# Gate projection by block products in one more group, chunks outermost in the output stage, and PSUM banks by due time

## Chip, core and metric

The kernel runs on one core of a Trainium2 chip. The metric is device time in microseconds (us) of one execution, lower is better. The time before is 316.57 us, the median of 4 runs (316.33 to 316.61).

## What is computed

The kernel chains a linear attention with cosine weights and a gated feed-forward block. There are 8 batches, 8 heads, 576 positions and a head size of 64, so 4608 tokens of 512 features; the inner width is 1536.

```python
def phi(x, c, s):                       # c, s = cos, sin of pi/2 * pos / 576
    r = np.maximum(x, 0.0)
    return np.concatenate([r * c, r * s], axis=-1)
kv  = einsum('bhsf,bhsd->bhfd', phi(k), v)
z   = sum(phi(k), axis=2)
num = einsum('bhsf,bhfd->bhsd', phi(q), kv)
den = einsum('bhsf,bhf->bhs', phi(q), z)[..., None] + 1e-06
x   = (num / den).transpose(0, 2, 1, 3).reshape(4608, 512)
g   = x @ w_gate
out = (g / (1 + exp(-g)) * (x @ w_val)) @ w_out
```

## The kernel before

**Groups and tiles.** The 4608 tokens are cut into nine groups (`tg` 0 to 8) of 512 tokens, each of four tiles of 128. Group 0 is spelled out in a list of words; the other groups run in a loop. A group has a product stage of 12 blocks of 128 inner features (`fc`) and an output stage. Attention work is spread between the blocks: the tiles of group `tg + 1` are made while group `tg` is in its product stage.

**Order.** The kernel writes the order of the instructions by hand: each engine runs its instructions in the order in which the Python code issues them. Side work goes into a plan: `at(s, f)` puts a function at slot `s`, `slot(s)` runs what is there. A group has 16 slots, 12 in the product stage and 4 in the output stage.

**Gate and value.** In groups 1 to 6, `ffn_mm` (L564) makes gate and value of a block with four matmuls of 512 columns each; ScalarE takes silu of the gate (L570), VectorE (DVE) multiplies by the value into `ht` (L575). In the groups of `GATE` (7 and 8), `ffn_by_quarters` makes the gate of four blocks at a time from seven block products in place of eight, a scheme of Strassen's kind. It has three thirds (`u`), each with products on banks a, b, e and c (L621): b is copied from a and accumulates in several steps, DVE adds a saved product `m7` to it for c (L659), then adds b to `m7` (L668), and ScalarE takes silu of m7, c, a and b (L627). The value products stay four matmuls of 512 columns (L633), and DVE makes `ht` from both (L638, the gating product). The weights' sums come from `gate_weight_sum` (L597), the tokens' sums from `x_sum` (L605).

**Output.** From group 2 on, `out_by_quarters` makes the output the same way, with seven products of 12 matmuls of 256 columns (L786). Its operand sums are made on DVE by `token_sum` (L760, S1 to S4) and `weight_sum`. Evictions are L799, L801, L811, L816 and L827. In the last group, bank b of this stage is two banks.

**Attention.** For a batch, `phi_q` takes relu on ScalarE (L266) and weights on DVE (L283) into `r_q`, and two DMA transposes on SP (`qturn_dma`, L306) turn it into `phit`. `vmul` (L287) weights v; `kv_mm` (L333) multiplies; `kv_out2` (L356) copies it out. `a_tile2` (L448) makes a tile in two banks; `x_of` divides it (L458, L467, L471), and a DMA transpose on SP (L548) makes `xT`. Groups 7 and 8's tokens come from batches 6 and 7.

**Queues.** Loads from the second batch on go on POOL's queue. `load_behind` (L996) first runs a small POOL copy (L998) that reads the turned q of the batch before, so that the load waits for it. Stores (`store`, L708) go on SP's queue, between the DMA transposes; the last group's are split over SP and ScalarE's queue.

**PSUM.** There are eight banks, handed out by `take`. Before group 7 the one used longest ago is taken; from group 7 on (`loose`), a single bank is taken first so that a pair stays free, then by last use in the order of the code.

Of the kernel before, what the change touches and what calls it, by code (L numbers as in the profile page):

```python
# [18 lines left out]
def kernel(  # L19
# [31 lines left out]
    KH = KC // 2  # L51
    GATE = (7, 8)

# [22 lines left out]
    filled = [False] * 8  # L76
    loose = [False]

    def take(n, hold=None, fills=False, seeded=False):

        taken = {x for r in held.values() for x in r}
        if loose[0]:
            free = [b for b in range(8) if b not in taken]
            if n == 1:
                bs = [min((b for b in free if filled[b] or not seeded), key=lambda b: (
                    not any(x != b and x + 1 != b and x + 1 in free for x in free), used[b]))]
            else:
                b0 = min((b for b in free if b + 1 in free), key=lambda b: max(used[b:b + 2]))
                bs = [b0, b0 + 1]
            if hold is not None:  # L90
                held[hold] = bs
            for b in bs:
                filled[b] = fills or seeded
            touch(bs)
            return banks[:, bs[0]] if n == 1 else banks[:, bs[0]:bs[0] + 2]
        free = [b for b in range(0, 8, n) if not any(b <= x < b + n for x in taken)
                and (filled[b] or not seeded)]

        b0 = min(free, key=lambda b: (n == 1 and hold is not None and hold[0] == "o" and b ^ 1 not in taken,
                                      sorted(used[b:b + n], reverse=True)))  # L100
        if hold is not None:
            held[hold] = range(b0, b0 + n)
        filled[b0:b0 + n] = [fills or seeded] * n
        touch(range(b0, b0 + n))
        return banks[:, b0] if n == 1 else banks[:, b0:b0 + n]

    def touch(r):
        now[0] += 1
        for x in r:
            used[x] = now[0]  # L110

    def give_back(hold):
        touch(held.pop(hold))

# [162 lines left out]
    def phi_q(b, g):  # L277

        if g == 0:
# [4 lines left out]
                                in1=tab, op=ALU.mult)  # L284

    def vmul(b, g):
        nc.vector.tensor_tensor(  # L287
# [52 lines left out]
    def kv_out(b, engs=("act", "dve"), js=slice(0, J)):  # L340
        ps = st[b, "kvps"]
        for e, eng in enumerate(engs):
            for i in range(2):
# [3 lines left out]
                    in_=ps[hs, e, js.start * 2 * D1:js.stop * 2 * D1].rearrange("p (y x) -> p y x", x=D1))  # L347

    kv2s = [consts.tile([P, 2, J, 2, D1], BF16, name=f"kv2_{j}") for j in range(2)]

    def kv_out2(b):

        ps = st[b, "kvps"][:, :, 0:4 * J * D1 // 2].rearrange("p e (j w x) -> p e j w x", j=J, w=2)
        for w, eng in enumerate((nc.scalar.copy, nc.vector.tensor_copy)):
            for i in range(2):
                eng(out=kv2s[b % 2][w * D:(w + 1) * D, :, :, i], in_=ps[i * D:(i + 1) * D, :, :, w])  # L356

    def kv_free(b):
        give_back(("kv", b))

# [75 lines left out]

    def a_tile2(t):

        (b0, c0), (b1, c1) = (divmod(2 * t + r, NC) for r in range(2))
        ps = take(2)  # L440
        if b0 == b1:
# [3 lines left out]
        for e in range(2):  # L445
            for g in range(G):
                for ms, b, c, n in parts:
# [4 lines left out]
                    )  # L452
        x_of(t, ps)

# [152 lines left out]
    def ffn_by_quarters(tg, slot_of):  # L607
# [6 lines left out]

        def free(nm):
            give_back(("g", tg, nm))

        def product(to, u, a, x, first):
            for i in range(2):
                for c in range(KH):  # L620
# [8 lines left out]
        def V(u, i, w):  # L629
            fc = 4 * u + 2 * i + w  # L630
            val[u, i, w] = take(1, ("v", tg, fc), fills=True)
            for kc in range(KC):
                nc.tensor.matmul(out=val[u, i, w], lhsT=wv_sb[:, kc, fc * P:(fc + 1) * P], rhs=xT[tg][:, :, kc],  # L633
                                 start=(kc == 0), stop=(kc == KC - 1))

        def mul(u, i, w):
            fc = 4 * u + 2 * i + w
            nc.vector.tensor_tensor(out=ht[:, fc], in0=gates[u, w][:, i], in1=val.pop((u, i, w)), op=ALU.mult)  # L638
            give_back(("v", tg, fc))

# [4 lines left out]
        for u in range(3):  # L645
# [7 lines left out]
            nc.scalar.copy(out=m7, in_=e)  # L653
            free("e")
            V(*((u - 1, 1, 1) if u else (u, 0, 0)))
            done()
            product(b, u, W2, X2, False)
            c = bank("c", seeded=True)
            nc.vector.tensor_tensor(out=c, in0=m7, in1=b, op=ALU.add)  # L659
            product(a, u, A12, B21, False)  # L660
            silu(u, 1, 0, a)
            free("a")
            if u:
                mul(u - 1, 1, 1)
            V(u, 0, 0) if u else V(u, 1, 0)
            done()
            product(b, u, W1, X1, False)
            nc.vector.tensor_tensor(out=m7, in0=m7, in1=b, op=ALU.add)  # L668
            silu(u, 0, 1, m7)
            product(c, u, A22, X4, False)  # L670
            silu(u, 0, 0, c)
            free("c")
            V(u, 1, 0) if u else V(u, 0, 1)
            done()
            if u == 2:
                for n in (1, 2):
                    token_sum(n, 0, 4)
            mul(u, 0, 0)
# [4 lines left out]
            silu(u, 1, 1, b)  # L683
            free("b")
            if u:
                V(u, 0, 1)
            mul(u, 0, 1)
            if u:
                done()
                token_sum(*((3, 0, 4) if u == 1 else (4, 0, 4)))  # L690
        V(2, 1, 1)
# [29 lines left out]

    def ffn_out(t, f0=0, f1=None):

# [13 lines left out]
        else:  # L737
            nc.vector.tensor_single_scalar(out=ob_of(t), in_=ps, scalar=DOWN, op=ALU.mult)
        store(t)

# [26 lines left out]
    def out_by_quarters(tg, slot_of):  # L767

        last = tg == NTG - 1
        t0 = tg * OUT  # L770
        for t in (t0, t0 + 2):
# [11 lines left out]
        def product(to, a, b, first):  # L783
            for i in range(2):
                for kc in range(HC):
                    nc.tensor.matmul(out=to[i][:, 0] if len(to) == 2 else to[0][:, i],  # L786
# [28 lines left out]
        for p_, o_, x_ in each(b, c[0], C22):  # L815
            nc.vector.scalar_tensor_tensor(out=o_, in0=x_, scalar=UP, in1=p_, op0=ALU.mult, op1=ALU.add)  # L816
        token_sum(4, 4, 6)
        slot_of(0)
# [16 lines left out]
        else:  # L835
            for t in (t0 + 2, t0 + 3):
                store(t)
        slot_of(2)
# [3 lines left out]
        for t in (t0, t0 + 1):  # L842
            store(t, *((slice(HD, d_model), (nc.sync, nc.scalar)) if last else ()))
        slot_of(3)
# [151 lines left out]
    def load_behind(b):  # L996

        nc.gpsimd.tensor_copy(out=hold2, in_=phit[b - 1][0:1, :, 0, 0, 0])  # L998
        load(b, "q")
        if b > 3:  # L1000
            load_kv(b)

    def load_kv(b):
# [9 lines left out]
    for n in range(4):  # L1013
        at(SLOTS * (1 + n * (GATE[0] - 1) // 4) + FC + 3, lambda n=n: gate_weight_sum(n))
    for tg in GATE:
        for n in range(4):
            at(SLOTS * (tg - 1) + FC + (2, 2, 3, 3)[n], lambda tg=tg, n=(2, 0, 1, 3)[n]: x_sum(tg, n))
    for b in range(2, B):
        s0 = SLOTS * (b - 1)
        keng = "dve" if b == 2 else "act"  # L1020
        steps = [lambda b=b, g=g: phi_q(b, g) for g in range(G)]
        steps += [lambda b=b, g=g: (relu_k(b, g, g + 1, keng), vmul(b, g)) for g in range(G)]
        if b == 2:
            fs, tq = [s0 + i for i in (0, 0, 1, 1, 4, 5, 5, 6)], (s0 + 2, s0 + 2)
        else:
            p0 = s0 - SLOTS
            fs, tq = [p0 + 12, p0 + 12] + [p0 + 11 + i for i in range(2, 8)], (p0 + 15, p0 + 16)
            if b == 3:
                fs, tq = [p0 + 12 + i for i in range(4)] + [s0 + 4, s0 + 4, s0 + 5, s0 + 5], (s0 + 2, s0 + 2)
            at(p0 + 3 if b < 5 else p0 + 1, lambda b=b: load_behind(b))  # L1030
        tk = (s0 + 4, s0 + {2: 8, 3: 7}.get(b, 5))
        for s, f in zip(fs, steps):
            at(s, f)
        for e in range(2):
            at(tq[e], lambda b=b, e=e: qturn_dma(b, e))
        at(tk[-1], lambda b=b: kv_mm(b), lambda b=b: kv_out2(b))
        at(tk[-1] + 1, lambda b=b: kv_free(b))
    for t in range(2 * OUT, NTG * OUT):
        tg, i = divmod(t, OUT)
        s = SLOTS * (tg - 1) + (5 if tg > 2 else 4) + 2 * i  # L1040
        if t == 2 * OUT:
            at(s, a_(t, 0))
            at(s + 1, a_(t, 1), turn(t))
        elif tg == 2:
            at((9, 10, 11)[i - 1] + SLOTS, lambda t=t: a_tile2(t), turn(t))
            if i == 2:
                at(11 + SLOTS, load_3)
        else:
            if t in (13, 14, 15):
                s = SLOTS * 2 + t - 4  # L1050
            elif tg - 1 in GATE:
                s = SLOTS * (tg - 1) + ((1, 2, 7, 9) if tg < 6 else (1, 2, 4, 7) if tg < 8 else (1, 2, 5, 6))[i]
            at(s, lambda t=t: a_tile2(t), turn(t))
    for tg in range(1, NTG):
        s0 = SLOTS * tg
        if tg in GATE:
            loose[0] = True
            ffn_by_quarters(tg, lambda i: slot(s0 + i))
# [8 lines left out]
        for i in range(OUT):  # L1067
            ffn_out(tg * OUT + i)
            weight_sum(i)
# [32 lines left out]
```

## Time and profile before

| What | Value |
|---|---|
| median of 4 runs | 316.57 us |
| profiled execution | 316.33 us, span 314.6 us |
| granted TensorE clock | 0.997 |
| DVE busy | 228.5 us (73%) |
| ScalarE busy | 143.6 us (46%) |
| DMA reads and writes | 37.75 and 9.44 MB, 150 GB/s |

The page sums the busy time of each engine and follows back the chain of work that ended last: at each step to what released it, or to the instruction before it on its engine. A group of instructions is named by line, engine, operation and operands. Matmuls are pipelined: their ends are modelled, so the mean of one (379 ns for 512 columns) isn't what one costs in a stream, and a busy TensorE isn't TensorE at its peak. Waits are read from the chain in order of time and from the distances between starts. The windows view gives the busy time of each engine in a stretch of time; the timeline lists instructions with start, length and the idle time before them. Where DVE instructions follow without a gap, the lengths shown overlap a little, so the distance between starts is used for sums.

### The profile page before, as it was taken

The numbers are of one execution on the slowest core, as the hardware profiler recorded it, in microseconds if no ns is written. First come the engines' busy times: TensorE is split into PE (matmuls) and PEld (weight loads), VectorE is DVE, ScalarE is ACT, GpSimd is POOL, SyncE is SP. The second block draws the span as 40 slices with busy tenths as digits, with TensorE's granted clock in tenths as the row PEclk, the third lists the DMA queues.
The fourth block names the chain that finished last, engine by engine and source line by source line (L and its number), as shares of the span: only waits on it lengthen the run. The fifth ranks groups of instructions, "written<-read, shape, count | busy, mean of one in ns | idle before, by whom it ended". The sixth has DMA issues, their size and how long they took to land.

```text
span 314.6 us, 6775 instructions
## 1 busy us (share of the span) xinstructions
PE 307.3 (98%) x2696; PEld 189.7 (60%) x2696; DVE 228.5 (73%) x458; ACT 143.6 (46%) x264; POOL 36.2 (12%) x62
## 2 busy tenths in 40 slices
PE   8899999999999999999999999999999999999994
PEld 4597455445444585548654764577456866687673
DVE  7874777697678888587748786777779478945772
ACT  7554555763336356334543454335533345324530
POOL 7754202000200200030003000300000000000000
PEclk9999999999999999999999999999999999999998
DMA  7999998997797995999495969599951160014004
GB/s 255 222 198 197 206 205 138 230 136 102 136 208 118 148 147 120 142 118 201 95 151 75 200 141 156 73 188 138 161 89 35 38 147 17 20 36 99 0 2 133
DMA packets 74767, 41.07 MB, mean 131 GB/s; under 512 B 49904, under 2 KB 69872, under 8 KB 74736
## 3 DMA queue, kind: packets, MB, share of 16 engines
q1 hardware_dynamic: 51952, 22.55, 38.6%
q0 software_dynamic: 22192, 17.57, 37.3%
q10 hardware_dynamic: 592, 0.52, 0.5%
q8 instruction: 21, 0.34, 0.4%
q14 instruction: 10, 0.08, 0.1%
HBM read 37.75 MB, written 9.44 MB: 150 GB/s over the span
## 4 chain that ended last, share of the span: by engine, by line
PE 91%; DVE 5%; ACT 2%; issue 1%; ACTq 0%
PE banks L564 46%; PE banks L786 20%; PE banks L729 6%; PE banks L633 5%; PE banks L621 5%; PE banks L333 3%; PE banks L448 3%; DVE ht L638 1%; PE banks L494 1%; PE banks L430 1%; DVE v L287 1%; DVE sums L760 1%; DVE x L471 1%; PE banks L197 1%; PE banks L536 0%
## 5 line engine op out<-in xcount | busy, mean ns | idle before, releaser
L564 PE MATMUL banks<-xT,wg_sb 128*128 128x512 f16 (+2 forms) x368 | 86.6, 360 | 0.0
L564 PE MATMUL banks<-xT,wv_sb 128*128 128x512 f16 (+2 forms) x368 | 86.6, 360 | 0.0
L570 ACT ACTIVATE sg<-banks 128x512 bf16<-128x512 f32 (+2 forms) x92 | 51.5, 560 | 75.9 <-PE banks L564 73.9
L575 DVE TENSOR_TENSOR ht<-sg,banks 128x512 f16<-128x512 bf16 (+2 forms) x92 | 58.0, 637 | 29.7 <-PE banks L564 22.6
L564 PEld LDWEIGHTS <-wv_sb 128*128 128x128 f16 x368 | 35.5, 98 | 37.4
L564 PEld LDWEIGHTS <-wg_sb 128*128 128x128 f16 x368 | 33.9, 98 | 31.5 <-issue 0.2
L786 PEld LDWEIGHTS <-ht 128*128 128x128 f16 x336 | 32.5, 98 | 4.2
L786 PEld LDWEIGHTS <-sums 128*128 128x128 f16 x252 | 24.5, 98 | 4.2 <-issue 0.8
L633 PE MATMUL banks<-xT,wv_sb 128*128 128x512 f16 x96 | 24.3, 379 | 0.0
L283 DVE TENSOR_TENSOR r_q<-raw_q,tab 128x1152 bf16<-128x1152 bf16 x24 | 17.6, 754 | 7.4 <-ACT raw_q L266 7.1
L729 PE MATMUL banks<-wo_sb,ht 128*128 128x512 f16 x96 | 22.7, 379 | 0.0
L471 DVE TENSOR_TENSOR x<-banks,rec 128x512 f16<-128x512 f32 (+1 forms) x32 | 21.6, 674 | 1.3 <-PE banks L430 0.3
L786 PE MATMUL banks<-wo_sb,ht 128*128 128x256 f16 x168 | 20.6, 273 | 0.0
L287 DVE TENSOR_TENSOR v<-raw_v,tab 128x1152 bf16<-128x1152 bf16 x27 | 19.9, 753 | 0.4 <-ACT raw_v L849 0.4
L786 PE MATMUL banks<-wt_sb,sums 128*128 128x256 f16 x168 | 19.8, 273 | 0.1
L786 PE MATMUL banks<-wt_sb,ht 128*128 128x256 f16 x168 | 19.5, 273 | 0.0
L799 ACT ACTIVATE ob<-banks 128x512 f32<-128x512 f32 x14 | 8.4, 598 | 21.8 <-PE banks L786 21.8
L638 DVE TENSOR_TENSOR ht<-sg,banks 128x512 f16<-128x512 bf16 x24 | 15.5, 681 | 2.5 <-ACT sg L627 2.4
L266 ACT ACTIVATE raw_k<-raw_k 128x576 bf16<-128x576 bf16 (+1 forms) x25 | 17.0, 694 | 0.0
L998 POOL COPY hold<-phit 1x2 bf16<-1x2 bf16 x5 | 1.3, 268 | 129.0 <-DMA phit<-r_q 129.0
L760 DVE TENSOR_TENSOR sums<-ht 128x1024 f16<-128x1024 f16 (+1 forms) x28 | 15.5, 554 | 0.4
L266 ACT ACTIVATE raw_q<-raw_q 128x576 bf16<-128x576 bf16 x24 | 15.4, 674 | 0.0
(121 smaller groups left out, 335.0 us busy)
## 6 DMA issues: line engine op xcount, KB each, us to landing
out_dram<-ob SPq DMA_DIRECT2D x67, 128.0 KB, 2.4
raw_k<-in_k_dram POOLq DMA_DIRECT2D x7, 576.0 KB, 9.0
raw_q<-in_q_dram POOLq DMA_DIRECT2D x6, 576.0 KB, 6.1
raw_v<-in_v_dram POOLq DMA_DIRECT2D x6, 576.0 KB, 11.4
wo_sb<-in_moe_w_out_dram POOLq DMA_DIRECT2D x3, 512.0 KB, 13.0
wg_sb<-in_moe_w_gate_dram POOLq DMA_DIRECT2D x5, 256.0 KB, 8.9
wv_sb<-in_moe_w_val_dram POOLq DMA_DIRECT2D x5, 256.0 KB, 9.4
wo_sb<-in_v_dram SPq DMA_DIRECT2D x2, 576.0 KB, 4.1
```

The source lines that it names most:

```text
L266: nc.scalar.activation(out=out, in_=in_, func=AF.Relu)
L283: nc.vector.tensor_tensor(out=st[b, "q"][:, g], in0=o.unsqueeze(2).to_broadcast([P, NC, 2, D]), in1=tab, op=ALU.mult)
L287: nc.vector.tensor_tensor(out=v2s[b == 1][:, g, :, :, 0:D], in0=(first if b == 0 and g == 0 else {"v": raw_of(b, "v")})["v"][:, g].unsquee ...
L471: nc.vector.tensor_tensor(out=st["x", t].rearrange("p (y e d) -> p e y d", e=2, d=D)[:, :, ys], in0=ps[:, :, 0:2 * J * D1].rearrange("p e ...
L564: nc.tensor.matmul(out=st["f", tg, fc, lo][i], lhsT=(wg_sb, wv_sb)[i][:, kc, fs], rhs=xT[tg][:, ts, kc], start=(kc == 0), stop=(kc == KC - 1))
L570: nc.scalar.activation(out=sg[:, 0:n], in_=st["f", tg, fc, lo][0], func=AF.Silu, scale=DOWN)
L575: nc.vector.tensor_tensor(out=ht[:, fc, r:r + n], in0=st.pop(("s", tg, fc, lo))[:, 0:n], in1=ps[1], op=ALU.mult)
L633: nc.tensor.matmul(out=val[u, i, w], lhsT=wv_sb[:, kc, fc * P:(fc + 1) * P], rhs=xT[tg][:, :, kc], start=(kc == 0), stop=(kc == KC - 1))
L638: nc.vector.tensor_tensor(out=ht[:, fc], in0=gates[u, w][:, i], in1=val.pop((u, i, w)), op=ALU.mult)
L729: nc.tensor.matmul(out=o_ps[t], lhsT=ht[:, fc, r:r + P], rhs=wo_sb[:, fc], start=(fc == 0), stop=(fc == FC - 1))
L760: nc.vector.tensor_tensor(out=o[:, lo:hi], in0=x[:, lo:hi], in1=y[:, lo:hi], op=op)
L786: nc.tensor.matmul(out=to[i][:, 0] if len(to) == 2 else to[0][:, i], lhsT=a[:, kc, i * P:(i + 1) * P], rhs=b[:, kc], start=first and kc == ...
```

## The change

`GATE` becomes (6, 7, 8), so group 6 makes its gate by block products as well. In the output stage the two halves of a product are interleaved: the loop over chunks of the contraction (`kc`) is now outside the loop over token halves (`i`). The banks of the groups with block products are chosen by an estimate of when their last reader ends: `rows` counts TensorE's time in steps of about 10 ns, and `LATE` says how much later a bank is free. DVE's work on an attention tile that comes between the products of a third, and one half of the batch product's copies, are put on a list (`behind`) that is run after L659 or L668. The slots of phi_q, the transposes, the weighting of v and the tiles are tables (`ROW`, `TILES`). Batch 7's q is weighted by ScalarE in 18 activations with a scale, with no work on DVE. The q of batches 6 and 7 is loaded a group earlier, behind the loads of the batch before. Stores of groups 1 to 7 go on POOL's queue. S4 is summed wholly in the output stage in the groups of `GATE`, and in the closing third S1, S3 and S2 stand in another order.

```diff
-    GATE = (7, 8)
+    GATE = (6, 7, 8)
+    AHEAD = 6
+    WSUM = (31, 47, 63, 79)
+    ROW = {2: ((16, 16, 17, 17), 18, (20, 21, 21, 22), 8), 3: ((12, 13, 14, 15), 18, (20, 20, 21, 21), 7),
+           4: ((12, 12, 13, 14), 15, (15, 16, 17, 18), 5), 5: ((8, 9, 12, 12), 13, (13, 14, 15, 16), 5),
+           6: ((6, 8, 9, 12), 13, (13, 14, 15, 16), 3), 7: ([4 + i // 2 for i in range(18)], 13, (12, 13, 14, 15), 3)}
+    TILES = {2: (0, 9, 10, 11), 3: (5, 9, 10, 11), 4: (5, 7, 9, 11), 5: (2, 4, 7, 9), 6: (2, 4, 7, 9), 7: (0, 1, 5, 7), 8: (0, 3, 5, 7)}
+    LATE = dict(M=44, V=87, O=131, X=26, x=150, v=(190, 250, 120, 150), e=130, a=90, c=170, b=110, k=120)
...
-                bs = [min((b for b in free if filled[b] or not seeded), key=lambda b: (
-                    not any(x != b and x + 1 != b and x + 1 in free for x in free), used[b]))]
+                bs = [min((b for b in free if filled[b] or not seeded), key=lambda b: used[b])]
...
-    def touch(r):
+    def touch(r, late=1):
         now[0] += 1
+        if loose[0]:
+            for x in r:
+                used[x] = rows[0] + late
+            return
         for x in r:
             used[x] = now[0]
...
+    def phi_q_part(b, c, w):
+        if (b, "q") not in st:
+            st[b, "q"] = rel.tile([P, G, NC, 2, D], BF16, name="r_q")
+        nc.scalar.activation(out=st[b, "q"][:, :, c, w], in_=raws[b, "q"][:, :, c], func=AF.Relu,
+                             scale=csk[:, c, w:w + 1])
...
+        part(0, nc.scalar.copy)
+        if b - 1 in GATE:
+            behind.append(lambda: (part(1, nc.vector.tensor_copy), kv_free(b)))
+        else:
+            part(1, nc.vector.tensor_copy)
...
+        if later:
+            behind.append(lambda: (x_of(t, ps), give_back(("a2", t), LATE["x"]), x_turn(t)))
+        else:
+            x_of(t, ps)
+            give_back(("a2", t), LATE["x"])
...
             nc.vector.tensor_tensor(out=c, in0=m7, in1=b, op=ALU.add)
+            while behind:
+                behind.pop(0)()
             product(a, u, A12, B21, False)
             silu(u, 1, 0, a)
-            free("a")
-            if u:
-                mul(u - 1, 1, 1)
+            free("a", LATE["a"])
...
             nc.vector.tensor_tensor(out=m7, in0=m7, in1=b, op=ALU.add)
+            while behind:
+                behind.pop(0)()
             silu(u, 0, 1, m7)
+            if u:
+                mul(u - 1, 1, 1)
...
+        queues = (nc.gpsimd, nc.gpsimd) if tg > 0 else None
...
-            for i in range(2):
-                for kc in range(HC):
+            rows[0] += LATE["O"]
+            for kc in range(HC):
+                for i in range(2):
...
-        token_sum(4, 4, 6)
+        token_sum(4, 0 if tg in GATE else 4, 6)
...
-        load(b, "q")
+        if b < AHEAD:
+            load(b, "q")
         if b > 3:
             load_kv(b)
+        if AHEAD <= b + 1 < B:
+            load(b + 1, "q")
...
+            later = tg - 1 in GATE and s in (0, 1, 3, 4, 7, 8)
+            at(SLOTS * (tg - 1) + s, lambda t=t, later=later: (a_tile2(t, later), None if later else x_turn(t)))
```

## The prediction

> **What bounds the kernel now.** I read the engine shares first, then the chain of waits in order of time, then the windows of the last three groups.
>
> ```profile
> PE 307.3 (98%) x2696; PEld 189.7 (60%) x2696; DVE 228.5 (73%) x458; ACT 143.6 (46%) x264; POOL 36.2 (12%) x62
> ...
> PE 91%; DVE 5%; ACT 2%; issue 1%; ACTq 0%
> ```
>
> TensorE is on the chain for 91% of the span, so a cut of its columns shows one for one, unless another engine then holds it. The chain says what a column costs and where TensorE is held already:
>
> ```profile
> 217.91 10.36 PE banks L564 x48
> ...
> 241.07 9.28 PE banks L786 x84
> 250.34 0.87 PE banks L621 x8
> 251.22 0.86 PE banks L633 x4
> ...
> 256.54 0.70 DVE x L471
> 257.29 0.60 PE banks L621 x4
> ...
> 266.99 0.70 DVE banks L659
> 267.73 0.61 PE banks L621 x4
> ...
> 274.44 0.44 DVE sums L760
> 274.92 6.29 PE banks L786 x56
> ```
>
> 48 matmuls of 512 columns take 10.36 us, 216 ns each; 8 of 256 columns 0.87 us, 109 ns each. In the ordinary group 6 (217.8 to 250.2) the chain stays on PE. In group 7, which has the block products, it runs through DVE from about 264 to 275.
>
> ```profile
> core 0: us, PE busy (x) PEld busy (x) DVE busy (x) ACT busy (x) POOL busy (x), PEclk, DMA share, GB/s
> 250.18:281.05 30.87, 30.37 (x251) 22.03 (x249) 22.95 (x45) 12.27 (x22) 0.00 (x0) 1.00 0.24 52
> 281.05:309.90 28.85, 28.85 (x218) 20.97 (x215) 19.17 (x34) 12.19 (x23) 0.00 (x0) 1.00 0.21 51
> 217.75:250.18 32.43, 32.43 (x294) 19.65 (x292) 23.30 (x45) 12.44 (x22) 0.00 (x0) 1.00 0.48 86
> ```
>
> By counts group 7 needs 84 x 0.109 (gate) + 48 x 0.216 (value) + 4 x 0.26 (attention tiles) + 84 x 0.109 (output) = 29.76 us. It takes 30.87, so 1.1 us are waits: on x (a bank), on another bank at 263.7, on L659, and on the last sums. "PE busy" hides most of them, since ends are modelled.
>
> **Group 6, gate by block products.** Out go 48 matmuls of 512 columns (10.36 us), in come 84 of 256 (9.18 us): -1.2 us. Value product, batch product (1.18 us) and four attention tiles stay. Here a rule speaks against the change. The Trainium skill (TensorE: Matmul & The Clock Gate, "Back-to-back issue gap") gives about 81 ns per matmul at 128 columns and 131 ns at 512 for a sustained stream of weight load and matmul. A straight line between them, my estimate, gives 98 ns at 256: 8.2 us against 6.3, a loss of 1.9 us. The chain has 109 and 216 ns, with the 98 ns weight loads hidden, so I take -1.2; the measurement decides.
>
> What it asks of DVE in group 6's product stage, by start-to-start times of group 7's rows: 12 gating products at 0.62 (three in 1.87 us), 3 pairs L659/L668 at 1.4, 4 tiles at 1.04 (den, rec, x), the batch copies 0.87, token sums 3.4: about 20 us against 21.9 of PE. That fits only if the order is right, so I followed the new order of each engine product by product, with these durations. (T is the first product of a third of the stage.)
> - First third: the last v product (0.75 us, behind the ScalarE relu) now stands before the first L659; it ends near T+2.4, and L659's input comes at T+2.7. No wait.
> - The new order defers the tile's den/rec/x behind L659 and L668, so L659 and L668 start when their product ends. The value product in the first tile's bank wants it at T+4.9; x ends near T+4.4.
> - Second third, with the batch product: L659 ends at T+4.2, the product over the same bank comes at T+4.7.
> - Last third: PE's products end at T+7.76 (seven at 0.437, five value products at 0.864, a tile over two batches at 0.38), then the output's a, e and b (S2) follow at 1.31 each, so b begins at 10.4. DVE: L659 2.8 to 3.4, x to 4.5, L668 to 5.2, gating product 5.8, S1 6.5, two gating products 7.7, S3 8.2, gating 8.8, S2 9.4, last gating 10.1, the two remainders 11.0. With i outermost S2's last chunks are wanted at 10.8; with chunks outermost at 11.2.
>
> So group 6 should be free of new waits, but by 0.2 to 0.4 us at several places. I take 0.1 us; bounds 0 and 1.1 (what group 7 lost).
>
> **Group 7.** S4's first four chunks (0.69) leave the closing chain for the output stage, where nothing wants S4 for 3 us; sums are wanted 0.44 us later; tiles no longer stand before L659. This removes the waits at 257.3, 267.7 and 274.9. One wait appears, as I read the banks that the new choice gives out: the second tile of group 7's stage (after the second third's first value product) takes the bank of the third value product of the first third. By the chain's durations the first third ends at 5.91 us (seven products, three value products, one tile), and a, e and a value product later, at 7.65, the tile wants it. Its gating product is the last of three:
>
> ```profile
> 257.15 1.87 DVE L638 TENSOR_TENSOR ht<-sg,banks 128x512 f16<-128x512 bf16 x3
> ```
>
> L668 starts at 4.43 (its product ends at 4.17), ends at 5.12; silu of m7, then of bank c, is done 1.1 us later (255.87 to 256.95 in the trace), 6.25; the three products end near 8.15. TensorE waits 0.5 us. The end assumed in `LATE` fits the later thirds, where another value product comes first. Sum for group 7: 1.1 - 0.5 = -0.6, bounds -1.1 and 0. Group 8 has no tiles; its 28.85 against 28.7 by count gives -0.15.
>
> **Chunks outermost, at the end.** In the last group the final product has two banks. With i outermost the first half is done early, and its eviction and stores run beside the second half:
>
> ```profile
> 309.43 0.42 DVE L801 TENSOR_SCALAR ob<-banks 128x256 f32<-128x256 f32 x1 [1.54 <-PE banks L786]
> 310.08 1.50 ACTq L711 DMA_DIRECT2D out_dram<-ob  x2
> ...
> 310.09 0.42 DVE L801 TENSOR_SCALAR ob<-banks 128x256 f32<-128x256 f32 x1 [0.23 <-PE banks L786]
> ```
>
> With chunks outermost both halves end together: the first eviction starts near 310.0, 0.55 us later. ScalarE's queue holds two stores of 0.75 us back to back, so the last one moves as much. If the issue isn't what counts, only the second eviction does: +0.3. I take +0.5.
>
> **The rest, near nothing.**
> - q of batch 7 by ScalarE: 18 activations of 256 columns (nearest row 0.38 to 0.40 us) for 4 relus of 0.67, two per block of 1.73 us beside a silu of 0.60: 1.4 of 1.73, and 3 us off DVE. Uncovered, silu would be late by one of them, under the 0.86 us until its value product ends.
> - phi_q of batches 5 and 6 inside groups 3 and 4: 0.75 each on DVE (24.2 busy of 32.6 there). By the same walk the closing sums end about 26.2 us into group 4, wanted at 26.5. Bounds 0 and 0.3 each.
> - weight sums earlier, 0.95 us each on DVE in output stages: no wait.
> - Loads: q of batch 5 still comes in its own group, and is now wanted at block 8, 17.3 us into group 3. It waits on POOL for q's transposes: today they start 5 us into the group behind eight stores and release the copy at 15.5; without the stores I get 11.3, and with 5.9 us to landing 17.4. ScalarE may stand for half a microsecond; TensorE feels it from about 20. q of batches 6 and 7 comes a group earlier.
> - Stores of groups 1 to 7 on POOL: 56 issues of about 0.75 us on an engine 12% busy. The Trainium skill (DMA: Bandwidth & Descriptors, "SWDGE vs HWDGE vs iDMA") sends plain transfers to SP or ACT, and warns that GpSimd writes descriptors into SBUF from which VectorE can lock it out. The rows show no price: POOL's issue at 203.72 takes 0.77 us, and the L760 beside it 0.69, as elsewhere. A store has some 25 us until its buffer is written again: 0.
>
> ```profile
> 203.72 0.77 POOL L131 DMA_DIRECT2D raw_v<-in_v_dram  x1
> ...
> 203.82 0.69 DVE L760 TENSOR_TENSOR ht<-ht 128x1024 f16<-128x1024 f16 x1
> ```
>
> **Sum.** -1.2 + 0.1 - 0.6 - 0.15 + 0.5 = -1.35 against 316.33 of the profiled execution (span 314.6): 315.0. The runs' median lies 0.24 above that execution; half of this gives **315.1**, own range 314.5 to 315.8.
>
> **Rivals.**
> - *All waits go* (0.16): group 7's bank is free in time and the tail costs 0.3: -1.2 - 1.1 - 0.15 + 0.3 = -2.15, 314.3. For it: the choice by due time is made for this. Against: three gating products in 1.87 us can't end sooner.
> - *Group 6 stalls as group 7 did* (0.15): +1.1 in place of 0.1 gives 316.1. For it: margins of 0.2 us. Against: the new order removes what stalled group 7.
> - *DVE becomes the bound of group 6* (0.09, the slower side): if group 6 pays group 7's 1.1 and what it has besides, the v product and the batch copies (0.75 + 0.87), it loses 2.7; if the same backlog keeps group 7's waits, the change is -1.2 + 2.7 - 0.15 + 0.5 = +1.85: 318.3. It decides from 1.2 us of backlog behind L659 on; 20 us of work in 21.9 speaks against it.
> - *q of batch 5 is late* (0.02): every microsecond beyond 20 is lost on TensorE after the eight banks fill.
> - It does nothing in group 6: not possible, the 84 products stand in PE's order.
>
> About 0.2% (0.63 us) is what a measurement of this kernel can tell from no change. From the cases: the first two are faster almost wholly, the third is mostly within; faster 0.76, within 0.14, slower 0.10. The range 314.2 to 316.5 leaves out the slower rivals, a part of the third, and the lower edge of the second.
>
> **What would show it.** Group 6 from first gate product to the next group's: 31.1 to 31.3 us (32.43). Group 7: 30.2, with one wait of 0.5 us of an attention tile on the gating product; if that is missing, the first rival. At the end: both evictions after the last matmul, the last stores 0.5 us later. Waits of PE on DVE in group 6 beyond 0.5 us, or a group 7 at 30.9, make it wrong; so does a wait of ScalarE on raw_q beyond 2 us in group 3.

## The result, and the profile after

The changed kernel takes 318.09 us, the median of 42 runs (316.37 to 323.06); the kernel before takes 316.69 us on the same chips. The ratio is 1.0044, 95% interval 1.0033 to 1.0055: slower by 0.44%, where 0.5% faster was forecast. The ratios here leave out executions more than 1.5% above the quickest of their kernel (322.73 and 323.06 us of the changed one), the medians and ranges hold all. The profiled execution is one of the quickest of the changed kernel: 316.66 us, span 314.9.

The first view of the page after is the busy time of the engines and the head of the chain of waits:

```profile
PE 304.4 (97%) x2732; PEld 193.4 (61%) x2732; DVE 230.2 (73%) x461; ACT 150.5 (48%) x284; POOL 65.6 (21%) x118
...
PE 16%; DVE 0%; DVEq 0%; issue 0%
```

TensorE is busy for 2.9 us less than before and the span has not shrunk, so something waits. The chain can't say where: in this trace it is followed back no further than 259 us. The windows do, here from each group's first gate product to the next group's (groups 3, 4, 6, 7 and 8; after the stretch a row has its length, then TensorE's busy time):

```profile
core 0: us, PE busy (x) PEld busy (x) DVE busy (x) ACT busy (x) POOL busy (x), PEclk, DMA share, GB/s
...
120.31:155.01 34.70, 32.54 (x287) 19.76 (x285) 26.55 (x49) 15.61 (x29) 7.24 (x14) 1.00 0.94 155
155.01:187.43 32.42, 32.42 (x294) 19.63 (x292) 24.74 (x46) 14.82 (x28) 6.64 (x13) 1.00 0.93 144
...
219.63:250.87 31.24, 31.24 (x331) 23.15 (x328) 24.36 (x47) 13.62 (x26) 4.20 (x9) 1.00 0.43 72
250.87:281.19 30.32, 29.89 (x251) 22.16 (x248) 22.72 (x44) 12.23 (x22) 4.15 (x9) 1.00 0.24 53
281.19:309.89 28.70, 28.70 (x218) 21.04 (x215) 18.60 (x32) 12.18 (x23) 3.93 (x8) 1.00 0.18 49
```

Groups 6 and 7 are where the forecast had them (31.1 to 31.3, and 30.2). Group 3, which the forecast had unchanged, is 2.3 us longer. TensorE's waits (in total, times, longest, in us) show one new one that is long and one of 0.4:

```profile
PE banks L825 <- DVE x L500: 2.0, 1, 2.0
PE banks L429 <- DVE wgs_sb L421: 1.3, 1, 1.3
...
PE banks L473 <- DVE ht L669: 0.4, 1, 0.4
```

The one at L429 is in the start-up. It was 0.4 us before, and costs nothing: group 3 starts at 120.31 us, before at 120.28. The timeline of group 3 shows what the long one consists of (start, length, engine, line and operation; in brackets the idle time before it and what ended that):

```profile
121.12 11.31 SPq L323 DMA_TRANSPOSE phit<-r_q  x2
...
133.88 0.17 POOL L1037 COPY hold<-phit 1x2 bf16<-1x2 bf16 x1 [9.79 <-DMA phit<-r_q]
134.38 0.79 POOL L142 DMA_DIRECT2D raw_q<-in_q_dram  x1 [0.32 <-issue]
...
141.39 0.68 ACT L277 ACTIVATE raw_q<-raw_q 128x576 bf16<-128x576 bf16 x1 [3.75 <-DMA raw_q<-in_q_dram]
142.10 0.76 DVE L294 TENSOR_TENSOR r_q<-raw_q,tab 128x1152 bf16<-128x1152 bf16 x1 [2.65 <-ACT raw_q L277]
...
145.08 0.69 DVE L500 TENSOR_TENSOR x<-banks,rec 128x512 f16<-128x512 f32 x1
...
145.82 1.47 PE L825 MATMUL banks<-wo_sb,ht 128*128 128x256 f16 x12 [2.02 <-DVE x L500]
```

Read it upwards from the last row. The first output product wants a bank that still holds an attention tile; DVE frees it with the x that starts at 145.08. DVE is late because it stood 2.65 us at L294, which wants relu of batch 5's q; ScalarE made that at 141.39, after standing 3.75 us for the load. The load was issued at 134.38, behind the small POOL copy that waits for the transposes of batch 4's q. Their row is 11.31 us long for two, and from its start to the copy it is 12.8 us. The same rows of the kernel before:

```profile
125.38 7.88 SPq L306 DMA_TRANSPOSE phit<-r_q  x2
...
135.99 0.17 POOL L998 COPY hold<-phit 1x2 bf16<-1x2 bf16 x1 [30.87 <-DMA phit<-r_q]
136.44 0.74 POOL L131 DMA_DIRECT2D raw_q<-in_q_dram  x1 [0.28 <-issue]
```

Before, the pair's row is 7.88 us long, and the copy comes 10.6 us after its start. The load was issued two us later still than after, but the relus of this q stood four blocks further on, at 146.62, and nothing waited. The last rows that answer to the forecast are those of the end:

```profile
309.98 0.76 DVE L840 TENSOR_SCALAR ob<-banks 128x256 f32<-128x256 f32 x2 [1.86 <-PE banks L825]
...
310.50 1.43 ACTq L748 DMA_DIRECT2D out_dram<-ob  x2
```

Both evictions now run after the last product, as foretold, and the rows of the last stores end at 311.93, before at 311.58.

The table has the distances between the starts of the last output products of successive groups, and, as the tail, from the last of these starts to the end of the last store's row. It holds two further executions of the changed kernel and three kernels of the experiments below.

| us | before | after | after again | after again | phi5_back | put_together | put_together_2 |
|---|---|---|---|---|---|---|---|
| execution | 316.33 | 316.66 | 319.71 | 322.17 | 314.33 | 313.79 | 313.62 |
| group 3 | 32.39 | 34.70 | 36.44 | 39.48 | 32.39 | 32.39 | 32.39 |
| group 4 | 32.63 | 32.42 | 32.42 | 32.43 | 32.43 | 32.43 | 32.43 |
| group 5 | 32.45 | 32.20 | 33.39 | 32.82 | 32.29 | 32.20 | 32.20 |
| group 6 | 32.43 | 31.24 | 31.24 | 31.24 | 31.24 | 31.23 | 31.23 |
| group 7 | 30.87 | 30.32 | 30.32 | 30.32 | 30.32 | 29.87 | 29.87 |
| group 8 | 28.84 | 28.70 | 28.70 | 28.70 | 28.70 | 28.84 | 28.70 |
| tail | 3.00 | 3.35 | 3.34 | 3.35 | 3.35 | 3.14 | 3.13 |

From before to after: 2.31 - 0.21 - 0.25 - 1.19 - 0.55 - 0.14 + 0.35 = +0.32, and the executions differ by 0.33.

### The profile page after: what moved, and what is told of

It is laid out like the page before. It is cut to its first block, busy times and chain, and to the rows that moved or that the text cites. A ratio compares the mean times of both kernels' runs of the same rounds, so it can differ in the third digit from the quotient of the medians.

```text
span 314.9 us, 6868 instructions
## 1 busy us (share of the span) xinstructions
PE 304.4 (97%) x2732; PEld 193.4 (61%) x2732; DVE 230.2 (73%) x461; ACT 150.5 (48%) x284; POOL 65.6 (21%) x118
## 5 line engine op out<-in xcount | busy, mean ns | idle before, releaser
L593 PE MATMUL banks<-xT,wg_sb 128*128 128x512 f16 (+2 forms) x320 | 74.3, 358 | 0.0
L593 PE MATMUL banks<-xT,wv_sb 128*128 128x512 f16 (+2 forms) x320 | 74.3, 358 | 0.0
L599 ACT ACTIVATE sg<-banks 128x512 bf16<-128x512 f32 (+2 forms) x80 | 44.1, 554 | 54.0 <-PE banks L593 50.6
L604 DVE TENSOR_TENSOR ht<-sg,banks 128x512 f16<-128x512 bf16 (+2 forms) x80 | 49.8, 630 | 27.1 <-PE banks L593 16.9
L748 POOL DMA_DIRECT2D out_dram<-ob x56 | 29.4, 532 | 122.0 <-ACT ob L838 117.3
L593 PEld LDWEIGHTS <-wv_sb 128*128 128x128 f16 x320 | 30.8, 98 | 31.7
L664 PE MATMUL banks<-xT,wv_sb 128*128 128x512 f16 x144 | 36.5, 379 | 0.0
L669 DVE TENSOR_TENSOR ht<-sg,banks 128x512 f16<-128x512 bf16 x36 | 23.3, 681 | 3.3 <-ACT sg L657 3.1
L657 ACT ACTIVATE sg<-banks 128x512 bf16<-128x512 f32 x27 | 15.2, 590 | 10.8 <-PE banks L651 10.8
L664 PEld LDWEIGHTS <-wv_sb 128*128 128x128 f16 x144 | 14.1, 98 | 9.9
L294 DVE TENSOR_TENSOR r_q<-raw_q,tab 128x1152 bf16<-128x1152 bf16 x20 | 14.7, 753 | 6.1 <-ACT raw_q L277 6.0
L651 PEld LDWEIGHTS <-wgs_sb 128*128 128x128 f16 x144 | 13.5, 98 | 5.4
## 6 DMA issues: line engine op xcount, KB each, us to landing
wo_sb<-in_moe_w_out_dram POOLq DMA_DIRECT2D x3, 512.0 KB, 12.8
```

Of the source, the lines that this page charges most:

```text
L593: nc.tensor.matmul(out=st["f", tg, fc, lo][i], lhsT=(wg_sb, wv_sb)[i][:, kc, fs], rhs=xT[tg][:, ts, kc], start=(kc == 0), stop=(kc == KC - 1))
L599: nc.scalar.activation(out=sg[:, 0:n], in_=st["f", tg, fc, lo][0], func=AF.Silu, scale=DOWN)
L604: nc.vector.tensor_tensor(out=ht[:, fc, r:r + n], in0=st.pop(("s", tg, fc, lo))[:, 0:n], in1=ps[1], op=ALU.mult)
L651: nc.tensor.matmul(out=to[:, i], lhsT=a[:, c, 2 * u + i], rhs=x[:, :, c], start=first and i == 0 and c == 0, stop=c == KH - 1, skip_group_ ...
L657: nc.scalar.activation(out=gates[u, w][:, :, j * HT:(j + 1) * HT], in_=src, func=AF.Silu, scale=DOWN)
L748: (queues or (nc.sync, nc.sync))[e].dma_start(out=out_v[idx // NC, idx % NC][:, cols], in_=ob_of(t)[e * SH:(e + 1) * SH, cols])
```

## The experiments

Two theories stood at the start. **The late load** (A in the expectations below): the relus of batch 5's q were moved ahead of the arrival of their data; ScalarE, DVE and TensorE stand one behind the other. **The stores** (B): 56 stores on POOL's queue disturb loads and transposes, and the late load is only where that shows first. A third, that group 6 or the new loop order costs what the page doesn't show (C), is answered by the same runs. All diffs are against the changed kernel unless they say otherwise.

**q5_ahead: load batch 5's q a group earlier, too.**

```diff
-    AHEAD = 6
+    AHEAD = 5
```

> The changed kernel, with the q of batch 5 loaded a group ahead too (as 6 and 7 are). Theory A (the q of batch 5 is loaded in the same group that now weights it at block 8; ScalarE stands in its order for the load, the silus and VectorE behind it, TensorE after that): the 3.7 us wait of ScalarE on raw_q in group 3 and the 2.0 us wait of TensorE go, group 3 takes 32.4 instead of 34.7 us, and the time falls to about 314.8 (ratio to before near 0.994), with a spread as small as that of the kernel before. Theory B (stores on POOL collide with the DMA transposes and slow everything that waits on DMA): little changes, above 316.5, spread stays at 3 us. Theory C (group 6 or the interleaved output loop costs what the page doesn't show): no change.

315.71 us, ratio to before 0.9968 (0.9956 to 0.9980). ScalarE no longer waits for that load. Group 3 still takes 33.31 us, since the loads that now go first make TensorE wait 0.9 us at the group's start for a turned token tile (xT), which lands in 7.0 to 9.2 us where it took 3.4 to 7.5. And a second wait of the same build shows in group 5; its timeline:

```profile
200.12 0.18 POOL L1037 COPY hold<-phit 1x2 bf16<-1x2 bf16 x1 [10.10 <-DMA phit<-r_q]
200.12 0.91 ACT L300 ACTIVATE r_q<-raw_q,cs_all 128x256 bf16<-128x256 bf16 x2 [3.92 <-DMA xT<-x]
...
206.48 1.02 PE L593 MATMUL banks<-xT,wg_sb 128*128 128x512 f16 x4 [0.72 <-DVE x L500]
```

L300 is batch 7's q on ScalarE. It writes `r_q`, of which the kernel has a single buffer, and starts just as the POOL copy says that the transposes of batch 6's `r_q` are done (in the first profile 200.31 and 200.30), so I take these for the cause, not the xT that the row names. ScalarE stands 3.92 us, and again TensorE ends up waiting for x.

**stores_sp: all stores back on SP's queue.**

```diff
-        queues = (nc.gpsimd, nc.gpsimd) if tg > 0 else None
+        queues = None
...
-            ffn_out(tg * OUT + i, queues=(nc.gpsimd, nc.gpsimd))
+            ffn_out(tg * OUT + i)
```

> The changed kernel with all stores on SP's queue, as before. Theory A: the transposes of batch 4's q stand behind eight stores again and release the POOL copy near 15.5 us into group 3 instead of 13, so that the q of batch 5 lands later and TensorE loses more: slower than the changed kernel by 1 to 3 us, 319 or more. Theory B: the transposes get their 7.5 to 7.9 us a pair back (11.3 now), landings fall to 2.4 us for stores and 2.8 for xT: faster than the changed kernel by over 1 us.

319.86 us, ratio 1.0095 (1.0068 to 1.0123): worse, not better. The pair of transposes is back at 7.88 us, and at 10.6 us to the copy, but it starts 4.2 us later behind the eight stores, at 125.29. So the load is issued at 136.31 and ScalarE stands 4.8 us. That the stores are on POOL is not the cause of the loss; it softens it.

**phi5_back: batch 5's q at the blocks where it was.**

```diff
-           4: ((12, 12, 13, 14), 15, (15, 16, 17, 18), 5), 5: ((8, 9, 12, 12), 13, (13, 14, 15, 16), 5),
+           4: ((12, 12, 13, 14), 15, (15, 16, 17, 18), 5), 5: ((12, 12, 13, 14), 15, (15, 16, 17, 18), 5),
```

> The changed kernel with batch 5's phi_q back in the output stage (slots 12, 12, 13, 14, transposes at 15, weighting of v at 15 to 18), its load as it is. Theory A: the load has some 8 us more, the waits in group 3 go, time near 314.8 to 315.2. Theory B: no gain beyond 0.3 us.

315.11 us, ratio 0.9948 (0.9934 to 0.9963). Group 3 is back at 32.39 us. All of TensorE's waits, the first, second and fourth of them in the start-up:

```profile
PE banks L208 <- DVE zeros L203: 1.0, 1, 1.0
PE banks L454 <- DVE wt_sb L442: 0.6, 1, 0.6
PE banks L473 <- DVE ht L669: 0.4, 1, 0.4
PE banks L429 <- DVE wgs_sb L421: 0.2, 1, 0.2
```

One table entry takes the loss away, with the stores left on POOL.

**before_phi5_early: that entry alone, put into the kernel before.**

```diff
+            if b == 5:
+                fs[0:4], tq = [p0 + 8, p0 + 9, p0 + 12, p0 + 12], (p0 + 13, p0 + 13)
             if b == 3:
```

> The kernel before with this one cause added: batch 5's phi_q at blocks 8 and 9 and twice at 12, its transposes at 13, everything else as before (stores on SP, q loaded in its own group). Theory A: ScalarE stands for raw_q in group 3, from 17.3 to about 21.5 us into it, TensorE loses 3 us or more: 319.5 or more, with a wide spread. Theory B or C: within 0.3 us of before.

322.10 us, ratio 1.0125 (1.0100 to 1.0150, without two of the six executions, of 324.2 us). ScalarE stands 5.3 us for the load and group 3 takes 37.98 us. With no store on POOL and no other part of the change, the entry makes the loss by itself, and a larger one, since the load is issued later there (137.44) and the clock falls behind the stall (table below).

**after_look_1 and after_look_2: the changed kernel, profiled twice more.** Its times spread over 6.7 us, and the profile so far is of a quick one.

> The changed kernel as it is, profiled again. Its profile so far is of one of its quickest executions (316.66 us, where the median is 318.09). If the spread of its times is the wait for the q of batch 5, a longer execution shows ScalarE waiting longer for that load than 3.7 us, and group 3 longer than 34.7 us by the same amount, with the other groups as they were. If the spread is something else (the granted clock, say), group 3 stays at 34.7 us and the other groups are longer, each by about the same share.

> The same once more, as executions differ: by the first theory, time less 316.66 us equals ScalarE's wait for that load less 3.7 us, within 0.4 us; by the second the wait stays at 3.7 us.

They took 319.71 and 322.17 us. The sum expected failed: ScalarE's wait for the load is 3.9 and 5.9 us, 0.2 and 2.1 us longer than in the first profile, while the executions are 3.05 and 5.51 us longer. The table has the difference in groups 3 and 5 alone (1.74 + 1.19 and 4.78 + 0.62), so it isn't a clock that is lower throughout. The windows of after_look_1 around TensorE's stall show what is missing (length, busy time of TensorE and its matmuls, then its granted clock):

```profile
144.00:146.00 2.00, 0.01 (x1) 0.96 1.19 196
146.00:149.30 3.30, 3.27 (x16) 0.51 1.22 207
149.30:152.00 2.70, 2.70 (x27) 1.00 0.89 166
```

and of after_look_2:

```profile
144.00:146.60 2.60, 0.58 (x8) 1.00 1.24 192
146.60:153.50 6.90, 5.49 (x27) 0.51 1.02 170
153.50:156.00 2.50, 2.50 (x25) 1.00 0.20 40
```

The clock is granted at half for 3.3 us from the end of the stall in after_look_1, and for 6.9 us in after_look_2, there from 1.4 us before the stall's end. In the first profile it stays at 1.00 all through. The price can be read from the timeline: from the start of the first output product to that of the third takes 3.93 us in the first profile (145.82 to 149.75), 5.48 in after_look_1 (146.03 to 151.51) and 6.58 in after_look_2 (148.01 to 154.59), so 1.55 and 2.65 us are clock. Without them, group 3's loss against 32.39 us lines up with ScalarE's wait:

| kernel | ScalarE's wait | loss of group 3 | of it clock | rest | wait less rest |
|---|---|---|---|---|---|
| after | 3.75 | 2.31 | 0 | 2.31 | 1.44 |
| after_look_1 | 3.92 | 4.05 | 1.55 | 2.50 | 1.42 |
| stores_sp | 4.76 | 3.33 | 0 | 3.33 | 1.43 |
| before_phi5_early | 5.32 | 5.59 | 1.73 | 3.86 | 1.46 |
| after_look_2 | 5.88 | 7.09 | 2.65 | 4.44 | 1.44 |

The first 1.44 us of the wait cost nothing, and each us beyond costs one on TensorE, with the clock on top. Group 5 follows the same form with the wait for batch 6's transposes: a wait of 2.7, 3.0, 3.6, 3.9 and 4.1 us (after, phi5_back, tail_halves, q5_ahead, after_look_1) goes with 32.20, 32.29, 32.90, 33.22 and 33.39 us, so its free part is about 2.9. Three more traces lie on the same line: 3.4, 3.5 and 3.85 us with 32.68, 32.82 and 33.14 (g6_back, after_look_2, halves_all).

**phi5_back_sp: phi5_back with all stores on SP.** The base of this and the next kernels is phi5_back, and the diff is that of stores_sp.

> The kernel with batch 5's q back where it was (315.1 us), and all stores on SP's queue again, none on POOL's. It asks what the move of the stores is worth where nothing waits for the q of batch 5. If POOL's stores are what slows the transposes (a pair took 7.9 us before, 11.3 us after), the pair of batch 5 is back near 8 us and nothing is lost: 315.1. If SP has no room for the stores ahead of its transposes, these come later, the wait of ScalarE for batch 7's (3.0 to 3.9 us so far) grows, and above some 3.2 us TensorE loses as much as it grows by: 315.5 to 317.

316.90 us, ratio 1.0009 (0.9992 to 1.0026): 1.8 us more than phi5_back. The size is that of the second case, the place isn't: ScalarE's wait for batch 7's is gone, and the loss is in group 4 (34.53 us, 2.1 more than in phi5_back). It has two parts, a wait for xT at the group's start and one for the transposes of batch 5's q, with which SP's queue is late:

```profile
151.95 6.24 SPq L748 DMA_DIRECT2D out_dram<-ob  x8
...
153.65 1.04 PE L593 MATMUL banks<-xT,wg_sb 128*128 128x512 f16 x4 [0.86 <-DMA xT<-x]
...
158.29 7.71 SPq L323 DMA_TRANSPOSE phit<-r_q  x2
...
170.51 0.32 PE L473 MATMUL banks<-kv,phit 128*64 128x65 bf16 x7 [0.80 <-DMA phit<-r_q]
```

In phi5_back this pair starts at 153.35, since no store stands ahead of it on SP; its row is 11.22 us long there, and the POOL copy that waits for it still comes 2.7 us sooner (167.92 against 170.62). The xT is issued at nearly the same time in both (146.01 and 145.93) and lands at 153.60 for 152.29. Beside it run the loads of group 3, which went out 1.7 us later here (136.28 for 134.55) behind the transposes of batch 4's q; that they delay it is likely and not shown.

**g6_back: group 6's gate by whole-row products again.**

```diff
-    GATE = (6, 7, 8)
+    GATE = (7, 8)
```

> The kernel with batch 5's q back where it was (315.1 us), and group 6's gate projection by whole-row products again, as in the kernel before. It sizes the first term of the forecast. Sum: 48 products at 216 ns for 84 at 109 ns are 1.2 us more on TensorE, so about 316.3, with group 6 at 32.3 to 32.4 us instead of 31.2. If the block products gained only because group 6 had waits before, group 6 stays within 0.3 us of 31.2 and the time within 315.1 to 315.4.

315.63 us, ratio 0.9967 (0.9955 to 0.9979). Group 6 takes 32.43 us where the base has 31.24: 1.19 us, against 1.2 by count. The medians differ by only 0.52, in part because group 7 is 0.19 us shorter here (30.13); the base's own six runs lie between 314.33 and 315.86, mostly by the wait in group 5 if its profile speaks for them, so the group is the better measure.

**tail_halves and halves_all: the halves one after the other in the last group's two-bank products, and in all output products.**

```diff
-            for kc in range(HC):
-                for i in range(2):
+            for kc, i in sorted(((kc, i) for kc in range(HC) for i in range(2)), key=lambda y: y[::-1] if len(to) == 2 else y):
```

> The kernel with batch 5's q back where it was (315.1 us), and in the last output product alone the halves one after the other again, so that the first half's closing sum runs beside the second half's products. Sum: the first sum starts 0.55 us earlier and the stores with it, so 0.4 to 0.5 us less, 314.6 to 314.7. If the last store's landing is set by the second half alone, the first half's lead is worth nothing: 315.1.

> The kernel with batch 5's q back where it was (315.1 us), and the halves one after the other in every output product of the output stage, as in the kernel before. If the loop order is worth something only at the end, this equals the kernel with the halves one after the other in the last product, 314.6 to 314.7. If chunks outermost helps in the groups before the last (a wait for the last chunk of the gated product falls behind both halves' first chunks), each group start after group 2 pays 0.1 to 0.3 us here, and it is 315.1 to 316.

In halves_all the new line lists i outermost without a condition. tail_halves takes 314.95 us, ratio 0.9943 (0.9928 to 0.9959), halves_all 315.81, ratio 0.9971 (0.9958 to 0.9985). tail_halves has a tail of 3.13 us in place of 3.35 and loses 0.13 of the 0.22 in group 8: it undoes the order in a product that waits for DVE's last closing sum, too. That product in the timeline of tail_halves:

```profile
300.40 2.92 PE L824 MATMUL banks<-wt_sb,sums 128*128 128x256 f16 x24
```

and in that of phi5_back:

```profile
299.67 2.78 PE L825 MATMUL banks<-wt_sb,sums 128*128 128x256 f16 x24
```

It is 2.92 in the kernel before as well. halves_all takes 32.76, 31.37 and 30.45 us in groups 4, 6 and 7, tail_halves 32.42, 31.23 and 30.33. So chunks outermost is worth 0.34, 0.14 and 0.12 us there, and 0.14 in group 8, as I read it because the last chunk of a late sum is wanted after both halves' first chunks instead of in the middle; no row names that wait.

**put_together and put_together_2.** The first has phi5_back, the loop of tail_halves, a due time for the bank behind the wait of 0.4 us that fits its use, and batch 7's q two blocks later. The second has the halves one after the other in the very last product alone.

```diff
-            give_back(("v", tg, fc), LATE["v"][2 * w + i])
+            give_back(("v", tg, fc), LATE["v"][2 * w + i] + (LATE["V"] if fc == 1 else 0))
...
-           6: ((6, 8, 9, 12), 13, (13, 14, 15, 16), 3), 7: ([4 + i // 2 for i in range(18)], 13, (12, 13, 14, 15), 3)}
+           6: ((6, 8, 9, 12), 13, (13, 14, 15, 16), 3), 7: ([6 + i // 2 for i in range(18)], 15, (12, 13, 14, 15), 3)}
```

> A version meant to beat both: batch 5's q where it was, the halves one after the other in the last product, the bank of the third gating product of group 7 given a due time as late as it is used, and batch 7's q work two blocks later. Sum from 315.1: 0.45 off at the end, 0.43 off where TensorE waited for that bank at 259 us, nothing for ScalarE's wait of 3 us, which TensorE did not feel: 314.2, profiled execution 313.4 to 313.6. If the bank that takes the place of the late one is late itself, the wait of 0.4 us stays at another product: 314.6.

> The version put together (314.1 us) with the halves one after the other in the very last product alone; the product of the last group with the second table's sums, which took 2.92 us with the halves one after the other and 2.78 us with chunks outermost, has chunks outermost again. Sum: 0.14 off, 313.95. If the 0.14 us is given back at the last product, it stays at 314.1.

314.10 us, ratio 0.9917 (0.9904 to 0.9930), and 313.82 us, ratio 0.9902 (0.9887 to 0.9918); one of the four executions of the second took 318.39 us, was not profiled and is not in the ratio. Group 7 falls by 0.45 us to 29.87, group 5 is at 32.20, and in the second group 8 is at 28.70 with the tail still 3.13. In put_together_2 TensorE waits only in the start-up; its list of waits in full:

```profile
PE banks L208 <- DVE zeros L203: 1.0, 1, 1.0
PE banks L454 <- DVE wt_sb L442: 0.6, 1, 0.6
```

By the medians it is faster than both kernels: by 2.9 us than the one before, measured beside it.

## Why the prediction was wrong

**Most terms came out; one that was put at nothing decided.** The prediction gave 315.1 us, and phi5_back, which is the change without the early q of batch 5, takes 315.11. That these agree to a hundredth is luck: the profiled execution of phi5_back is 314.33 where the sum had 315.0, mostly by 0.36 us in groups 4 and 5 and 0.15 in the tail, and its median lies 0.78 above that execution where the forecast added 0.12. The step that failed is the one on loads ("q of batch 5 still comes in its own group, and is now wanted at block 8"), and the rival *q of batch 5 is late*, given 0.02, is what happened: 2.3 us in group 3 in the quickest profile, more in the longer ones. Its parts, counted from the group's start at 120.31 us:
- **The release.** "Without the stores I get 11.3"; it came at 13.6. The stores had left SP's queue, but they still ran: POOL issued them from 119.90 to 124.09 us, beside the transposes, and the copy came 12.8 us after the start of these instead of 10.6. The walk moved the transposes forward and kept their length. stores_sp shows it: with the stores back on SP they take 10.6 again.
- **The landing.** 5.9 us assumed, 7.0 found (134.38 to 141.39), and of the 0.5 us from the copy to the issue of the load the sum has 0.2. Together 21.1 in place of 17.4.
- **The point.** "TensorE feels it from about 20." It is wanted at 17.3 and 1.44 us are free, so TensorE feels it from 18.8; from there to 21.1 are the 2.3 us that group 3 lost. I had counted eight banks to be filled; but the two engines behind ScalarE run in order, so one late relu held DVE's gating product and the x behind it, and with x one bank that TensorE wanted early. "Every microsecond beyond" was right as a price, and incomplete by the clock.
- **The chance.** With 17.4 against 17.3 the margin was already negative by my own walk, on a transfer whose landing times differ (5.7 to 6.2 us for four loads of q in the profile before). That was ground for a margin, not for 0.02: the landings found range from 6.0 to 8.5 us (stores_sp 136.31 to 142.31, after_look_2 135.07 to 143.58).

**Group 6, -1.2 + 0.1.** 31.24 for 32.43, and 1.19 back in g6_back. The walk through DVE's order held: no new wait. The rule of the skill weighed there would have made it a loss; the row decided rightly.

**Group 7, -0.6.** -0.55. The one wait foreseen is there, at the tile and at the gating product named, 0.43 us for 0.5. put_together's due time takes 0.45 us off, and the wait is gone from its list, which shows the cause.

**Group 8, -0.15.** -0.14, but not from what the count of a group without tiles had in mind: it is the loop order in the product with the last sum, as put_together (28.84) and put_together_2 (28.70) show.

**The tail, +0.5.** +0.35 from before to after. Undoing the order in the last product gives 0.22 of it back. What the forecast missed is the other side of the same edit: chunks outermost also takes waits out of the groups before, 0.34, 0.14, 0.12 and 0.14 us in halves_all against tail_halves and in group 8. Groups 4 and 5, taken as unchanged, are 0.21 and 0.25 us shorter; for group 4 the loop order covers it. In group 5 it isn't the loop order, since halves_all lies on the line of the wait there; which other part of the change it is, no run separates.

**Stores on POOL, 0.** Not 0, and not a loss: in the changed kernel's order of work, with batch 5's q put back, their return to SP costs 1.8 us. The issue takes 0.53 us, not the 0.75 of the larger loads.

**Batch 7's q on ScalarE, 0.** The activations take 0.50 us, not 0.38 to 0.40: the nearer row was the one of L504, which also scales by partition and took 0.48 for 260 columns. What I did not see is that they wait for batch 6's transposes, which read the only buffer of `r_q`. That cost nothing in the first profile and 1.2 us in after_look_1, since a wait of 2.7 us is under the free 2.9 and one of 4.1 is not.

**Above the quick execution.** The first profile is only 0.33 us above before, the median 1.4. The two further profiles show that longer executions differ by these two waits and the clock behind the first; runs at the median itself were not profiled.

## What to carry to other kernels

When work that starts with a load is moved to an earlier place, compare its new time of need with the landing, counted through every queue that the load waits behind, and treat a margin of nothing as a loss to be priced. An instruction that stands on an engine that runs in order holds all that is behind it, also what has nothing to do with the load, and the price appears on TensorE two engines further on as a bank that is not free. A stream that is moved to another queue frees that queue, but it still runs: here the transposes beside it took 11.3 us a pair for 7.9, and both effects belong in the sum.

## What was not expected of the hardware

- **A short stall can cost more than itself.** After a stall of 2.0 us, with 0.3 us of another just before, the clock was granted at half for 3.3 us; after stalls of 0.9, 0.6 and 2.0 us (before_phi5_early) it was so for 3.4, with 1.5, 0.6 and 2.0 for 6.9, from within the last of these; after 2.0 alone, and after 0.4, 0.6 and 2.0 in stores_sp, not at all. The Trainium skill (TensorE: Matmul & The Clock Gate, "Part 1: The HAM clock gate") tells of a free-running window of about 3.4 us after which the rate is halved or restored. Stretches of one and of two such lengths agree with that, and so does the chance in it; but the page asks for an idle window, and no idle time here is as long as 3.4 us; the traces decide. What sets it off in one execution and not in another stays open.
- **Stores beside DMA transposes.** In groups 3 and 4, with POOL's stores in flight, the row of a pair of transposes is 10.4 to 11.8 us long, with the stores on SP 7.6 to 8.7. The stores themselves, by the median of each trace, land in 4.1 to 5.3 us from POOL's queue (the eight of group 3 in 6.9 in the first profile) and in 2.4 to 2.5 from SP's. What the two share is not shown.
